# A fused attention and MoE kernel: the first gated products for one chunk of 128 tokens at a time

## The chip, the cores and the metric

The kernel runs on one core of one Trainium2 chip. The metric is the device time of one execution in microseconds (us). The engines are PE (matmul; its weight loads are listed apart as PEld), DVE and ACT (elementwise work, and the only ones here that empty PSUM), POOL (a few copies and products) and SP (issues the DMAs). Each engine takes its instructions in order; they meet at semaphores.

## The reference, cut to what matters

A delta-rule attention over 768 tokens, 4 batches, 8 heads of size 48, and then a gated MoE of one expert on all 3072 tokens:

```python
for t in range(S):
    kt, vt, bt = (k_n[:, :, t], v[:, :, t], beta[:, :, t, None])
    y[:, :, t] = np.einsum('bhd,bhde->bhe', q[:, :, t], state)
    v_old = np.einsum('bhde,bhd->bhe', state, kt)
    state = state + bt[:, :, :, None] * np.einsum('bhd,bhe->bhde', kt, vt - v_old)
...
a = x @ w_a            # x: 3072 x 384, w_a and w_b: 384 x 1536
b = x @ w_b
return (a * b @ w_out).astype(np.float32)
```

`x` is the attention's `y` with the heads side by side.

## The kernel before

**Attention.** The 768 time steps are cut into 24 chunks of 32 steps; a chunk of all 4 batches is 128 tokens. Chunks go in groups of four. For a group there are the Gram products of keys and queries (`gram`, on PE from `rawb`), a triangular solve on DVE over all four chunks at once (`solve`: some thirty short multiplies and subtractions on `b`, finished by small PE products `b,tt`, `b,kb` and `wr,xn`), and then, chunk after chunk, the recurrence (`steps`): the state's product with keys and queries (`sh,rawb`), DVE's `f`, the product `f,tt`, ACT's `u`, the state's update `S_ps<-u,kb`, the output product `u,at`, and `y`. From `y`, DVE and ACT make the chunk's gated input, in two halves of 16 bits, in `xb`. Chunk 2s and chunk 2s+1 lie side by side in one slot of `xb`: 256 columns, a pair.

**MoE.** The hidden width of 1536 is cut into 12 weight blocks of 128. A block is loaded from `in_w`, unpacked on DVE (one TENSOR_SCALAR and two SCALAR_TENSOR_TENSOR on 128x1152), scaled and split into high and low parts: for the first four blocks by small PE products with `zi`, `neg` and `negr` and ACT casts, for the others on DVE. A unit is one block for one pair (`moe`): two groups of nine matmuls, 128x128 weights against 256 columns, give a and b in one PSUM bank; ACT copies a (`a`), DVE multiplies (`g`), ACT and DVE split the product (`ghl`). Two units later (`LAG`), `moe_out` multiplies `ghl` with the block of `w_out`: three matmuls of 384 columns for each chunk, into one PSUM bank per chunk, which stays taken until the last block of the run.

The units of the first two pairs are queued in runs (`QUEUE`): pair 0 with blocks 0 to 5, pair 1 with 0 to 5, then the same with 6 to 8 and 9 to 11; partial sums lie in `acc`. Later pairs take all 12 blocks in one run. So the first unit needs chunk 0 and chunk 1.

**What sets the order.** The code only records operations (`Plan.add`). `Plan.order` then runs a list scheduler (`Plan.pack`) six times, with priorities from each pass's result run backwards, and keeps the best order by its own estimate; `issue` writes that order out. It hands out the six PSUM banks and models instruction fetch and the TensorE clock by fixed numbers. Where it sees PE idle in the first 60 us it writes fillers, matmuls on a tile of ones (`ones`, line 477), up to `SHY` ns ahead of the next operation. All recorded work has line 486, so the names of tiles tell the operations apart.

Of the kernel before, what the change touches and what calls it, by code (L numbers as in the profile page):

```python
# [17 lines left out]
AF = mybir.ActivationFunctionType  # L18
ALU = mybir.AluOpType
# [4 lines left out]
DM, FF = 384, 1536  # L24
C = 32
NCH = S // C
P = 128
KR = 112
GROUPS = [list(range(i, i + 4)) for i in range(0, NCH, 4)]
NG = len(GROUPS)  # L30
NFC = FF // P
# [8 lines left out]
def boost(o):  # L40
    return BOOST.get(o.stream + ("_pe" if o.stream == "moe" and o.eng == "PE" else ""), 0.0)
# [1 line left out]

EARLY = [(0, "k"), (2, "k"), (0, "r")]
NEXT = [(2, "r", 2, "k"), (0, "v", 0, "r"), (2, "v", 2, "r"), (0, "w", 2, "r"), (1, "w", 0, "v"), (2, "w", 2, "v"), (4, "k", 0, "w"), (4, "r", 1, "w"), (4, "v", 2, "w")]
QUEUE = [(0, [0, 1, 2, 3, 4, 5]), (1, [0, 1, 2, 3, 4, 5]), (0, [6, 7, 8]), (1, [6, 7, 8]), (0, [9, 10, 11]), (1, [9, 10, 11])]
LAG = 2
LEAD = 4
URGENCY = {"first": 5000, "prep0": 5000, "solve0": 5000, "steps0": 5000, "w0": 3000, "w1": 2500, "w": 1500, "prep1": 3000, "solve1": 3000, "steps1": 3000, "prep": 200, "solve": 600, "steps": 500, "moe": 800, "moe_pe": 300}
# [11 lines left out]
class Plan:  # L61
# [350 lines left out]
    MOVE = (1200.0, 1300.0)  # L412
    LOADED = (3500.0, 5600.0)
    BEGIN, IDLE, SINCE, UNTIL = 63, (50.0, 440.0), 1200.0, 60e3
    SHY, KEEP, GAIN, HEAT = 1500.0, 0.41, 0.42, (3.0, 430.0)

    def fetch(self, t, n, took, pos, come, dma):
        slip, come, known = 0.0, come[:], len(come)
# [14 lines left out]
    def order(self):  # L433


        self.link()
        ops = self.ops
        self.first = {o.eng: o for o in reversed(ops)}
        self.users = {}
        for o in ops:  # L440
            for b in o.banks:
                self.users[b] = self.users.get(b, 0) + 1
        self.succ = [[] for _ in ops]
        self.pred = [[] for _ in ops]
        for i, o in enumerate(ops):
            for j in o.deps:
                late = self.late(ops[j], o)
                self.succ[j].append((i, late))
                self.pred[i].append((j, late))
        pri, best = [o.pri - boost(o) - 1e12 * (o.stream == 'load') for o in ops], None  # L450
        for _ in range(self.PASSES):
            found = self.pack(pri)
            if found is None:
                break
            at, stop, done, total, bind = found
            if best is None or total < best[0]:
                best = (total, at, stop, done, bind)
            _, stop, _, total, _ = self.pack([-t for t in stop], True)
            pri = [k - 1e12 if o.stream == 'load' else total - t - boost(o) for k, (o, t) in enumerate(zip(ops, stop))]
        for o, o.at, o.end in zip(ops, best[1], best[2]):  # L460
            pass
        self.bind, self.fill = best[4]
        return best[3]
# [26 lines left out]
def tile_kernel(ctx, tc, kqt, kn, vn, begin, w, out):  # L490
    nc = tc.nc
    plan = Plan(nc)
    V, A, T, G, SP = (
        plan.engine(e, o)
        for e, o in (("DVE", nc.vector), ("ACT", nc.scalar), ("PE", nc.tensor), ("POOL", nc.gpsimd), ("SP", nc.sync))
    )
# [7 lines left out]
    def ring(p, name, n, shape, dt):  # L504
        tiles = [p.tile(shape, dt, name=f"{name}_{i}") for i in range(n)]
        used = [0]

        def get():
            used[0] += 1
            return tiles[(used[0] - 1) % n]  # L510

        get.tiles = tiles
        return get

    plan.pool = [psp.tile([P, 512], F32, name=f"bank{i}") for i in range(6)]
    att, abr, opr = (partial(lambda kind, n: plan.bank(kind, next(n)), kind, count()) for kind in range(3))
# [10 lines left out]
    ghr = ring(cst, "ghl", LAG + 1, [P, 2, 256], F32R)  # L527
    ar = ring(cst, "a", 2, [P, 256], F32)
    gr = ring(cst, "g", 2, [P, 256], F32)
# [70 lines left out]
    def halves(fc):  # L600
        return wh[:, fc].bitcast(F16).rearrange("p (l a) -> p l a", l=2), wo[:, fc]
# [49 lines left out]
    def wpart(m, j, fc, hl):  # L651
        o = (m * 3 + j) * P
        return halves(fc)[0][:, hl, o : o + P]

    facs = [None] * NCH
    xsub = [None] * (NCH // 2)
# [25 lines left out]
    acc = [one(f"acc{i}", [P, DM]) for i in range(4)]  # L682
# [26 lines left out]
    grams, rest = {}, []  # L709
# [316 lines left out]
    pend = []  # L1026
# [2 lines left out]
    def mm(*a, **k):  # L1029
        T.matmul(*a, **k)  # L1030

    def moe(s, fcs):
        xt = xsub[s]
        for fc in fcs:
            assert fc in whole
            ab = abr().rearrange("p (a n) -> p a n", a=2)

            plan.behind = set(opened[-1:] + closed[-LEAD:][:1] * (len(closed) >= LEAD))
            opened.append(len(plan.ops))
            for m in range(2):  # L1040
                n = 0
                with plan.group():
                    for j in range(3):
                        for l, rr in ((0, 0), (0, 1), (1, 0)):
                            T.matmul(
                                ab[:, m, :], wpart(m, j, fc, l), xt[:, rr, j, :], start=(n == 0), stop=(n == 8)
                            )
                            n += 1
            asb = ar()
            A.copy(asb, ab[:, 0, :])  # L1050
            g32 = gr()
            V.tensor_mul(g32, ab[:, 1, :], asb)
            ghl = ghr()
            A.copy(ghl[:, 0], g32)
            V.tensor_sub(ghl[:, 1], g32, ghl[:, 0].bitcast(F32))
            closed.append(len(plan.ops) - 1)
            pend.append((s, fc, ghl, fc == fcs[0], fc == fcs[-1]))
            if len(pend) > LAG:
                moe_out(*pend.pop(0))
            yield  # L1060

    ops = {}

    def moe_out(s, fc, ghl, first, last):
        if first:
            ops[s] = [opr()[:, 0:DM] for i in range(2)]
        for i in range(2):
            with plan.group():
                for n, (l, k) in enumerate(((0, 0), (0, 1), (1, 0))):
                    T.matmul(  # L1070
                        ops[s][i],
                        ghl[:, l, i * P : (i + 1) * P],
                        halves(fc)[1][:, k],
                        start=(first and n == 0),
                        stop=(last and n == 2),
                    )
            if last:
                c = 2 * s + i
                part = acc[c] if s < 2 else None
                final = fc == NFC - 1  # L1080
                ob = obs[c % 2] if final else part
                if part is not None and c in started:
                    V.scalar_tensor_tensor(ob, ops[s][i], facs[c], part, op0=ALU.mult, op1=ALU.add)
                else:
                    A.activation(ob, ops[s][i], AF.Copy, scale=facs[c])
                    started.add(c)
                if final:
                    SP.dma_start(out[c], ob)
# [12 lines left out]
    def run_all(gen):  # L1101
        for _ in gen:
            pass
# [5 lines left out]
    def merge(*streams):  # L1109

        todo = [[g_, n_, 0] for g_, n_ in streams]
        total_n = max(n_ for _, n_ in streams)
        for i in range(total_n):
            for t in todo:
                while t[2] * total_n <= i * t[1] and t[2] < t[1]:
                    next(t[0], None)
                    t[2] += 1
        for t in todo:
            if t[0] is not moes:
                run_all(t[0])  # L1120

    queue = []

    def moe_stream():
        while True:
            if queue:
                yield from moe(*queue.pop(0))
            else:
                yield

    moes = lab("moe", moe_stream())

    ws = [lab(f"w{i}", weights(i)) for i in range(len(PARTS))]
# [23 lines left out]
    run_all(ws[1])  # L1157
    queue.extend(QUEUE)
    run_all(ws[2])
# [8 lines left out]
    for g in range(1, NG):  # L1168
        n = len(GROUPS[g])
        if g < 2:  # L1170
            merge((st[g], 3 * n), (moes, 4 * n), (pr[g + 1], 2 + len(GROUPS[g + 1])))
        elif g + 1 < NG:
            next(pr[g + 1])
            merge((st[g], 3 * n), (moes, 4 * n))
            merge((pr[g + 1], 2 + len(GROUPS[g + 1])), (moes, 2))
        else:
            merge((st[g], 3 * n), (moes, 4 * n))
        queue.extend((s, list(range(NFC))) for s in range(GROUPS[g][0] // 2, GROUPS[g][-1] // 2 + 1))
        if g + 1 < NG:
            merge((sv[g + 1], 8), (moes, 8))  # L1180
    while queue:
# [3 lines left out]
    while pend:  # L1185
        moe_out(*pend.pop(0))
# [69 lines left out]
```

## Time and profile before

| | |
|---|---|
| median of 3 runs | 656.53 us (655.1 to 660.78) |
| the profiled execution | 658.43 us |
| its span, first to last instruction | 656.6 us |
| granted TensorE clock, mean | 0.961 |
| PE busy | 625.9 us of the span |
| first gated product of a pair | 77.76 us |
| state product of chunk 8 begins | 196.54 us |

A row of the profile has the line, the engine and the operation, then out<-in by tile names, partitions and elements; x counts instructions. In a list of groups busy us and mean ns follow, then the engine's idle time before them and what ended it; "issue" means that the profile shows nothing the engine waited for. In a timeline a row begins with start and length in us, and the square bracket is idle time before it. A row of stretches has begin and end, length, busy us and count for each engine, the granted clock of TensorE (1.00 is full), the busy share of the DMA engines and GB/s. One call of an fp32 matmul is two matmuls and two weight loads in the trace.

### The profile page before, as it was taken

Reading aid. Unit: us, or ns where it says so; the run is one execution under the profiler, and the core shown is the slowest. Engines: PE = TensorE matmul, PEld = TensorE weight load, DVE = VectorE, ACT = ScalarE, POOL = GpSimd, SP = SyncE. Lnnn points to the kernel's source line nnn. Section 1 sums busy time; section 2 is a strip of 40 time slices with the busy share of each in tenths; the row PEclk is TensorE's granted clock in tenths of the full one; section 3 lists DMA queues with packets and bytes.
Section 4 is the critical chain, followed back from the end, with each engine's and each line's share of the span. In section 5 each row is a group of like instructions: output and inputs, shape, how many; then the busy total and the mean of one; then the engine's idle time right before and its main releaser. Section 6 shows DMA issues by size and latency. Waiting matters only on the chain.

```text
span 656.6 us, 26617 instructions
## 1 busy us (share of the span) xinstructions
PE 625.9 (95%) x12184; PEld 535.3 (82%) x12184; DVE 404.8 (62%) x1059; ACT 270.4 (41%) x599; POOL 25.7 (4%) x62
## 2 busy tenths in 40 slices
PE   7788999998999999999999999999999999999997
PEld 6575688777788887888878888888888888888887
DVE  5796699768666995448965389754686533222222
ACT  4245684245445634323373234733324333232322
POOL 0000000000012200000020000200000000000000
PEclk8858799879999999999999999999999999999999
DMA  7837202212276000004300033000000000000000
GB/s 252 312 130 272 80 4 74 80 70 76 70 226 190 19 2 27 4 14 134 108 2 29 4 115 112 26 4 28 3 1 26 4 3 25 1 25 2 25 1 24
DMA packets 19824, 42.78 MB, mean 65 GB/s; under 512 B 1280, under 2 KB 4352, under 8 KB 19712
## 3 DMA queue, kind: packets, MB, share of 16 engines
q1 hardware_dynamic: 19712, 41.08, 18.9%
q8 instruction: 95, 1.56, 1.0%
q14 instruction: 17, 0.14, 0.1%
HBM read 36.36 MB, written 4.72 MB: 63 GB/s over the span
## 4 chain that ended last, share of the span: by engine, by line
PE 78%; DVE 12%; ACT 4%; issue 3%; ACTq 0%
PE bank L486 75%; DVE b L486 3%; PE S_ps L486 3%; DVE tmp L486 2%; ACT sqf L486 2%; DVE wh L486 1%; DVE ghl L486 1%; DVE late L486 1%; DVE g L486 1%; ACT ghl L486 1%; ACT tt L486 1%; ACT a L486 0%; DVE sc L486 0%; DVE ss L486 0%; DVE s L486 0%
## 5 line engine op out<-in xcount | busy, mean ns | idle before, releaser
L486 PEld LDWEIGHTS <-wh 128*128 128x128 f16 x2592 | 241.2, 98 | 50.6 <-issue 22.4
L486 PE MATMUL bank<-xb,wh 128*128 128x256 f16 x2160 | 259.8, 273 | 2.2 <-issue 2.2
L486 PE MATMUL bank<-wo,ghl 128*128 128x384 f32 x864 | 192.3, 356 | 0.6 <-issue 0.6
L486 PEld LDWEIGHTS bank<-wo,ghl 128*128 128x128 f32 x864 | 145.2, 190 | 4.8 <-issue 1.6
L486 ACT COPY a<-bank 128x256 f32<-128x256 f32 x144 | 53.6, 372 | 195.4 <-PE bank L486 195.3
L486 DVE TENSOR_TENSOR g<-bank,a 128x256 f32<-128x256 f32 x144 | 60.8, 422 | 114.8 <-ACT a L486 113.5
L486 DVE TENSOR_TENSOR ghl<-g,ghl 128x256 fp32r<-128x256 f32 x144 | 62.3, 432 | 35.0 <-ACT ghl L486 33.8
L486 ACT CAST ghl<-g 128x256 fp32r<-128x256 f32 x144 | 58.1, 404 | 60.4 <-DVE g L486 59.6
L486 PE MATMUL bank<-late,wh 128*128 128x256 f16 x432 | 52.0, 273 | 1.2 <-ACT u L486 1.2
L486 DVE TENSOR_TENSOR b<-b,tmp 128x31 f32<-128x31 f32 (+20 forms) x154 | 50.9, 330 | 2.8
L486 DVE TENSOR_TENSOR tmp<-b,b 128x31 f32<-128x31 f32 (+20 forms) x154 | 50.8, 330 | 2.9
L486 ACT ACTIVATE y<-bank,sc 128x384 f32<-128x384 f32 x24 | 14.0, 582 | 45.1 <-PE bank L486 42.8
L486 DVE SCALAR_TENSOR_TENSOR y<-bank,sc,y 128x384 f32<-128x384 f32 x23 | 14.2, 616 | 29.6 <-ACT y L486 29.6
L486 PEld LDWEIGHTS bank<-rawb 48*32 48x32 f32 x1280 | 21.2, 117 | 7.7 <-issue 3.7
L486 PE MATMUL bank<-rawb 48*32 48x64 f32 x1280 | 24.0, 232 | 3.3 <-DMA rawb<-in_kqt 3.3
L486 DVE TENSOR_TENSOR b<-bank,dc 128x256 f32<-128x256 f32 x24 | 14.5, 605 | 20.6 <-PE bank L486 17.1
L486 PEld LDWEIGHTS bank<-sh,rawb 48*64 48x64 f32 x1216 | 21.3, 144 | 6.7 <-issue 5.3
L486 PEld LDWEIGHTS bank<-f,tt 32*32 32x32 f32 x1472 | 17.9, 107 | 9.3 <-issue 5.5
L486 PE MATMUL bank<-sh,rawb 48*64 48x48 f32 x1216 | 23.9, 229 | 0.7 <-issue 0.7
L486 PE MATMUL bank<-u,at 32*32 32x48 f32 x1536 | 22.3, 206 | 1.9 <-issue 1.9
L486 PE MATMUL bank<-f,tt 32*32 32x48 f32 x1472 | 21.2, 206 | 2.5 <-issue 1.4
L486 DVE TENSOR_TENSOR f<-vnb,bank 128x384 f32<-128x384 f32 x38 | 19.9, 548 | 5.7 <-PE bank L486 5.1
(120 smaller groups left out, 552.8 us busy)
## 6 DMA issues: line engine op xcount, KB each, us to landing
late<-in_w SPq DMA_DIRECT2D x10, 1152.0 KB, 6.8
rawb<-in_kqt SPq DMA_DIRECT2D x12, 512.0 KB, 3.7
out<-late SPq DMA_DIRECT2D x24, 192.0 KB, 1.9
rawb<-in_kqt SPq DMA_DIRECT2D x4, 1024.0 KB, 7.0
vnb<-in_vn SPq DMA_DIRECT2D x10, 384.0 KB, 3.2
kb<-in_kn SPq DMA_DIRECT2D x9, 384.0 KB, 3.9
wh<-in_w SPq DMA_DIRECT2D x2, 1152.0 KB, 9.7
late<-in_kqt SPq DMA_DIRECT2D x4, 512.0 KB, 3.7
```

Of the source, the lines that this page charges most:

```text
L486: fn(*(self.place(a, lease) for a in args), **{k: self.place(a, lease) for k, a in kw.items()})
```

## The change

The queue now holds units of a pair, a block and the chunks (`parts`) that it covers. The first four units are half units: chunk 0 with blocks 0 and 1, then chunk 1 with the same two; the rest go on in pairs as before, blocks 2 to 5 of pair 0 first. A half unit has the same eighteen weight tiles against 128 columns, half the columns in `a`, `g` and `ghl`, and a second product for its one chunk. `moe_out` keeps its sums by chunk in place of by pair, opened by a chunk's first unit of a run and closed by its last. Matmuls of 128x256 on `xb` fall from 2160 to 2124, and 72 of 128x128 come; the second products stay 864.

Besides, `SHY` goes from 1500 to 500: fillers may reach nearer to the operation behind them. The lines in `order` change nothing: they would act where a pass of the scheduler finds no order, and all six find one.

```diff
-QUEUE = [(0, [0, 1, 2, 3, 4, 5]), (1, [0, 1, 2, 3, 4, 5]), (0, [6, 7, 8]), (1, [6, 7, 8]), (0, [9, 10, 11]), (1, [9, 10, 11])]
+BOTH = (0, 1)
+QUEUE = [[(0, 0, (0,)), (0, 1, (0,)), (0, 0, (1,)), (0, 1, (1,))] + [(0, b, BOTH) for b in (2, 3, 4, 5)]]
+QUEUE += [[(s, b, BOTH) for b in bs] for s, bs in ((1, range(6)), (0, (6, 7, 8)), (1, (6, 7, 8)), (0, (9, 10, 11)), (1, (9, 10, 11)))]
...
-    SHY, KEEP, GAIN, HEAT = 1500.0, 0.41, 0.42, (3.0, 430.0)
+    SHY, KEEP, GAIN, HEAT = 500.0, 0.41, 0.42, (3.0, 430.0)
...
             if found is None:
-                break
-            at, stop, done, total, bind = found
-            if best is None or total < best[0]:
+                stop, total = [float(k) for k in range(len(ops))], 0.0
+            else:
+                at, stop, done, total, bind = found
+            if found is not None and (best is None or total < best[0]):
+                best = (total, at, stop, done, bind)
+            if 0 is None or total < best[0]:
                 best = (total, at, stop, done, bind)
...
-    def moe(s, fcs):
-        xt = xsub[s]
-        for fc in fcs:
+    def moe(units):
+        for u, (s, fc, parts) in enumerate(units):
+            xt = xsub[s]
             assert fc in whole
-            ab = abr().rearrange("p (a n) -> p a n", a=2)
+            lo, n_t = parts[0] * P, len(parts) * P
+            ab = abr().rearrange("p (a n) -> p a n", a=2)[:, :, 0:n_t]
...
-                                ab[:, m, :], wpart(m, j, fc, l), xt[:, rr, j, :], start=(n == 0), stop=(n == 8)
+                                ab[:, m, :],
+                                wpart(m, j, fc, l),
+                                xt[:, rr, j, lo : lo + n_t],
+                                start=(n == 0),
+                                stop=(n == 8),
                             )
...
-            pend.append((s, fc, ghl, fc == fcs[0], fc == fcs[-1]))
+            mine = [2 * s + i for i in parts]
+            rest = [2 * v[0] + i for v in units[u + 1 :] for i in v[2]]
+            pend.append((fc, ghl, [(c, c not in sums, c not in rest) for c in mine]))
...
-    def moe_out(s, fc, ghl, first, last):
-        if first:
-            ops[s] = [opr()[:, 0:DM] for i in range(2)]
-        for i in range(2):
+    def moe_out(fc, ghl, work):
+        for i, (c, first, last) in enumerate(work):
+            if first:
+                ops[c] = opr()[:, 0:DM]
...
-        queue.extend((s, list(range(NFC))) for s in range(GROUPS[g][0] // 2, GROUPS[g][-1] // 2 + 1))
+        queue.extend([(s, fc, (0, 1)) for fc in range(NFC)] for s in range(GROUPS[g][0] // 2, GROUPS[g][-1] // 2 + 1))
```

The scheduler sorts the whole program anew, so much stands elsewhere. On ACT, around chunk 1's `u`, which the recurrence waits for (`wh`, `wo` and `sqf,sw` are the weight blocks, `sh` and `y` the recurrence), the order was

```order
L486 COPY u_74<-bank_63 128x384
L486 ACTIVATE wr_94<-bank_61 128x128
L486 CAST wh<-bank_62 128x384
L486 CAST wh<-bank_61 128x384
L486 ACTIVATE sqf,sw_138<-wh 128x768
L486 CAST wo<-bank_62 128x384
L486 COPY sh_76<-S_ps 112x768
L486 ACTIVATE y_96<-bank_64,sc_127 128x384
```

and now, on the same engine at the same place, it is

```order
L491 COPY u_74<-bank_63 128x384
L491 CAST wh<-bank_61 128x384
L491 COPY a_101<-bank_62 128x128
L491 CAST wh<-bank_63 128x384
L491 CAST ghl_98<-g_103 128x128
L491 ACTIVATE sqf,sw_138<-wh 128x768
L491 CAST wo<-bank_62 128x384
L491 COPY a_102<-bank_61 128x128
L491 CAST ghl_99<-g_104 128x128
L491 COPY sh_76<-S_ps 112x768
L491 ACTIVATE y_96<-bank_64,sc_127 128x384
```

Chunk 0's half units with blocks 0 and 1 now end ahead of chunk 2's `sh`, and `wr` of chunk 3's solve has moved behind chunk 2's `u`.

On PE, where the solve of group 1 (chunks 4 and 5: `b_3,tt_85` and `b_3,tt_86`) begins, second products stood between its parts:

```order
L486 MATMUL bank_64<-wo,ghl_99 128x384 x3
L486 MATMUL bank_63<-b_3_71,tt_85 32x16 x32
L486 MATMUL bank_62<-wo,ghl_99 128x384 x3
L486 MATMUL bank_66<-b_3_71,tt_86 32x16 x32
L486 MATMUL bank_63<-b_3_71,kb 128x256
L486 MATMUL bank_64<-wo,ghl_100 128x384 x3
L486 MATMUL bank_66<-b_3_71,kb 128x256
L486 MATMUL bank_63<-wr_93,xn 16x16 x32
```

and now the same engine has at this place

```order
L491 MATMUL bank_62<-wo,ghl_98 128x384 x3
L491 MATMUL bank_61<-wo,ghl_98 128x384 x3
L491 MATMUL bank_65<-b_3_71,tt_85 32x16 x32
L491 MATMUL bank_66<-b_3_71,tt_86 32x16 x32
L491 MATMUL bank_65<-b_3_71,kb 128x256
L491 MATMUL bank_62<-wo,ghl_99 128x384 x3
L491 MATMUL bank_66<-b_3_71,kb 128x256
L491 MATMUL bank_61<-wo,ghl_99 128x384 x3
```

The two `b,tt` groups have moved together; nine gated matmuls follow, and then the groups `wr_93,xn` and `wr_94,xn`, one right behind the other. Ahead of them PE now has six units of pair 0 and six of pair 1, where it had six and four.

At the start of PE's program the fillers stood as

```order
L477 MATMUL bank_66<-ones 128x256 x6
L486 MATMUL bank_61<-rawb 32x64 x32
L486 MATMUL bank_62<-rawb 32x64 x32
L486 MATMUL bank_63<-rawb 32x64 x32
L486 MATMUL bank_64<-rawb 32x64 x32
L477 MATMUL bank_66<-ones 128x256 x20
```

and are now

```order
L482 MATMUL bank_66<-ones 128x256 x7
L491 MATMUL bank_61<-rawb 32x64 x32
L491 MATMUL bank_62<-rawb 32x64 x32
L482 MATMUL bank_66<-ones 128x256
L491 MATMUL bank_63<-rawb 32x64 x32
L491 MATMUL bank_64<-rawb 32x64 x32
L482 MATMUL bank_66<-ones 128x256 x21
```

One filler more at either end and one between the Gram products of chunks 1 and 2; two others have moved in between the small products `sw,ones` of the first weight blocks, which makes 31 in place of 26.

More of the change, by code (lines that the diff above doesn't have):

```diff
@@ L1045, in moe @@
                             T.matmul(
-                                ab[:, m, :], wpart(m, j, fc, l), xt[:, rr, j, :], start=(n == 0), stop=(n == 8)
+                                ab[:, m, :],
[3 more added lines that the diff above has]
+                                stop=(n == 8),
                             )
                             n += 1
-            asb = ar()
+            asb = ar()[:, 0:n_t]
             A.copy(asb, ab[:, 0, :])
-            g32 = gr()
+            g32 = gr()[:, 0:n_t]
             V.tensor_mul(g32, ab[:, 1, :], asb)
-            ghl = ghr()
+            ghl = ghr()[:, :, 0:n_t]
             A.copy(ghl[:, 0], g32)
@@ L1056, in moe @@
             closed.append(len(plan.ops) - 1)
-            pend.append((s, fc, ghl, fc == fcs[0], fc == fcs[-1]))
+            mine = [2 * s + i for i in parts]
+            rest = [2 * v[0] + i for v in units[u + 1 :] for i in v[2]]
+            pend.append((fc, ghl, [(c, c not in sums, c not in rest) for c in mine]))
+            for c in mine:
+                sums.setdefault(c, None)
+                if c not in rest:
+                    over.add(c)
             if len(pend) > LAG:
                 moe_out(*pend.pop(0))
+            for c in over:
+                del sums[c]
+            over.clear()
             yield
-    ops = {}
-    def moe_out(s, fc, ghl, first, last):
-        if first:
-            ops[s] = [opr()[:, 0:DM] for i in range(2)]
-        for i in range(2):
+    sums, over, ops = {}, set(), {}
+    def moe_out(fc, ghl, work):
+        for i, (c, first, last) in enumerate(work):
+            if first:
+                ops[c] = opr()[:, 0:DM]
             with plan.group():
@@ L1070, in moe_out @@
                     T.matmul(
-                        ops[s][i],
+                        ops[c],
                         ghl[:, l, i * P : (i + 1) * P],
@@ L1077, in moe_out @@
             if last:
-                c = 2 * s + i
-                part = acc[c] if s < 2 else None
+                part = acc[c] if c < 4 else None
                 final = fc == NFC - 1
@@ L1082, in moe_out @@
                 if part is not None and c in started:
-                    V.scalar_tensor_tensor(ob, ops[s][i], facs[c], part, op0=ALU.mult, op1=ALU.add)
+                    V.scalar_tensor_tensor(ob, ops[c], facs[c], part, op0=ALU.mult, op1=ALU.add)
                 else:
-                    A.activation(ob, ops[s][i], AF.Copy, scale=facs[c])
+                    A.activation(ob, ops[c], AF.Copy, scale=facs[c])
                     started.add(c)
@@ L1126, in moe_stream @@
             if queue:
-                yield from moe(*queue.pop(0))
+                yield from moe(queue.pop(0))
             else:
```

## The prediction

> **What bounds the kernel now.** I read the page from the top: busy time by engine, the slices, the chain that ended last; then PE's busy time and granted clock in stretches cut where the clock changes; then PE's timeline where it stood still.
>
> ```profile
> PE 625.9 (95%) x12184; PEld 535.3 (82%) x12184; DVE 404.8 (62%) x1059; ACT 270.4 (41%) x599; POOL 25.7 (4%) x62
> PE   7788999998999999999999999999999999999997
> PEclk8858799879999999999999999999999999999999
> PE 78%; DVE 12%; ACT 4%; issue 3%; ACTq 0%
> q8 instruction: 95, 1.56, 1.0%
> L486 PEld LDWEIGHTS <-wh 128*128 128x128 f16 x2592 | 241.2, 98 | 50.6 <-issue 22.4
> L477 PE MATMUL bank<-ones 128*128 128x256 f32 x52 | 16.2, 484 | 1.1 <-DVE ones L486 1.1
> ```
>
> PE carries 78% of the chain and is busy 95% of the span: time can come only from PE's idle time, from PE at half clock, or from PE work left out. The slices put both losses in the first third. The stretches (us, PE busy, PEld, DVE, ACT, POOL, clock, DMA share, GB/s):
>
> ```profile
> 48.00:54.40 6.40, 6.40 (x136) 3.93 (x136) 2.62 (x12) 5.00 (x9) 0.00 (x0) 0.50 0.94 338
> 64.20:68.10 3.90, 1.19 (x9) 0.47 (x4) 2.06 (x7) 1.62 (x4) 0.00 (x0) 0.99 0.80 236
> 68.10:74.90 6.80, 6.76 (x72) 3.93 (x72) 5.23 (x9) 3.88 (x9) 0.00 (x0) 0.50 0.27 101
> 74.90:118.20 43.30, 42.90 (x1072) 37.05 (x1071) 38.21 (x119) 27.91 (x61) 0.00 (x0) 1.00 0.09 30
> 118.20:122.70 4.50, 3.12 (x135) 2.36 (x134) 4.50 (x8) 0.89 (x4) 0.00 (x0) 0.99 0.01 4
> 122.70:126.10 3.40, 3.40 (x72) 2.60 (x71) 3.40 (x4) 0.37 (x1) 0.00 (x0) 0.50 0.03 5
> 126.10:132.90 6.80, 6.31 (x158) 4.59 (x157) 2.72 (x10) 3.01 (x9) 0.00 (x0) 1.00 0.80 278
> 132.90:139.70 6.80, 5.45 (x140) 4.69 (x140) 2.19 (x7) 2.49 (x5) 0.00 (x0) 0.50 0.20 76
> 139.70:196.50 56.80, 54.30 (x1330) 46.23 (x1328) 41.31 (x84) 28.85 (x62) 2.25 (x10) 1.00 0.35 106
> 196.50:656.60 460.10, 450.20 (x7965) 393.04 (x7964) 260.18 (x703) 174.09 (x397) 20.77 (x39) 1.00 0.11 35
> ```
>
> And PE's timeline at the two kinds of loss, with DVE's row on which each chunk's gated input is complete:
>
> ```profile
> 48.17 0.56 DVE L486 TENSOR_TENSOR xb<-yt,xb 128x384 f16<-128x384 f32 x1
> 62.50 0.93 PE L486 MATMUL S_ps<-u,kb 32*48 32x48 f32 x64
> 63.37 0.88 PE L486 MATMUL bank<-u,at 32*32 32x48 f32 x64
> 66.78 0.34 PE L486 MATMUL bank<-wh,neg 128*128 128x384 f16 x1 [2.54 <-issue]
> 69.28 0.56 DVE L486 TENSOR_TENSOR xb<-yt,xb 128x384 f16<-128x384 f32 x1 [1.01 <-ACT xb L486]
> 77.76 2.13 PE L486 MATMUL bank<-xb,wh 128*128 128x256 f16 x18
> ...
> 106.53 2.14 PE L486 MATMUL bank<-xb,wh 128*128 128x256 f16 x18
> 108.42 1.30 PE L486 MATMUL bank<-wo,ghl 128*128 128x384 f32 x6
> ...
> 118.23 0.74 PE L486 MATMUL bank<-b,tt 32*32 32x16 f32 x64
> 118.90 0.79 PE L486 MATMUL bank<-wo,ghl 128*128 128x384 f32 x3
> 119.62 0.70 PE L486 MATMUL bank<-b,tt 32*32 32x16 f32 x61
> 121.70 0.24 PE L486 MATMUL bank<-b,tt 32*32 32x16 f32 x3 [1.38 <-issue]
> ```
>
> Chunk 0's input is complete at 48.7, chunk 1's at 69.8, and the first gated product runs at 77.76: for 29 us there is MoE work that could run, and doesn't. The stalls "issue" stand in the middle of a row of equal matmuls, so they wait for no data. 12184 matmuls and as many weight loads in 95 packets of the instruction queue are 256.5 instructions a packet: PE's instructions come in blocks of 128 pairs. The 128 pairs that end in the stall at 121.70 (64, 3, 61) need some 2.1 us of PE and took 3.47; those from 62.50 (64 and 64) need 1.75 and took 4.28, with DMA 0.80 busy. So PE can't get through a block faster than about 3.5 us, or 4.3 with transfers about, and after such a stall the clock fell to 0.50. The Trainium skill (Runtime: NRT & Kernel Launch, Instruction fetch mechanics) also has blocks of 256 instructions, but calls their fetch mostly hidden; the 1.38 us show that it isn't where tiles are small.
>
> **The change, part by part.** I compare PE up to one mark: the first product of chunk 8's step, 196.5 us before. Ahead of it both orders hold the same PE work, but for half groups and fillers. So the gain is the losses before the mark that vanish, less what is added and what is lost anew.
>
> Recovered, 64.2 to 74.9: idle 2.71 and 0.04, and half of 6.76 at clock 0.50, 3.38; together 6.1 us. In the new order the two groups that stalled (S_ps, u,at of chunk 1) stand between half groups and second products, so their block is long, PE has work where it waited, and nothing there lets the clock fall.
>
> Recovered, 118.2 to 196.5: idle 1.38, 0.49, 1.35 and 2.50, half clock 1.70 and 2.73; together 10.2 us. That all of it goes is not granted: what comes in its place is below.
>
> Added, half groups: 36 matmuls of 256 columns become 72 of 128. The wide one takes 105 ns (18 from 106.53 to 108.42), 3.8 us for 36. A narrow pair costs between half of that, 53 ns (0 more), and the 98 ns of its weight load (3.3 us more). As loads overlap matmuls in these rows I take the middle, 75 ns: 72 x 75 = 5.4, 1.6 more. The Trainium skill (TensorE: Matmul & The Clock Gate, Back-to-back issue gap) has some 81 ns for such a pair; the sum would be 0.4 us worse. No narrow pair is in this trace. The first nine run before 54.4 at clock 0.50: 9 x 75 = 0.7 more (0.5 to 0.9).
>
> Added, five more fillers on `ones` (two matmuls each). Three lie before 32 us, where PE waits for DVE anyway. Two stand between the small products of `sw` near 47 us, 2 x 2 x 484 ns = 1.9 us at most, where PE sat idle 0.9: I take 0.2 (0 to 1.0).
>
> Added waits: a half group waits for ACT's last cast of its half of the weight block, and behind it on PE, which runs in order, stands chunk 1's recurrence (f,tt and S_ps). For block 0's first half this cast is
>
> ```profile
> 52.90 0.48 ACT L486 CAST wh<-bank 128x384 f16<-128x384 f32 x1
> ```
>
> done at 53.4, and two other matmuls stand between it and the group, so I cost no wait; without them it would be the 0.5 us of the cast.
>
> Added on ACT and DVE: eight half evacuations on each, between the conversions of weight blocks 1 to 6. In this row DVE has 8.3 us free:
>
> ```profile
> 59.30:102.40 43.10, 39.45 (x1160) 30.23 (x1159) 34.78 (x85) 30.32 (x64) 0.00 (x0) 0.92 0.21 68
> L486 DVE TENSOR_SCALAR wh<-late x3: 751/753/754, 88.0 to 143.3; 128x1152 int32<-128x1152 int32 x3
> L486 DVE SCALAR_TENSOR_TENSOR wh<-late,wh x6: 1349/1352/1364, 98.3 to 146.3; 128x1152 int32<-128x1152 int32 x6
> L486 DVE TENSOR_TENSOR g<-bank,a 128x256 f32<-128x256 f32 x144 | 60.8, 422 | 114.8 <-ACT a L486 113.5
> ```
>
> Ahead of group 1's solve the order now has, on DVE, all of weight block 7 (0.75 + 2 x 1.35) and part of 8 (0.75 + 1.35), and two more units (4 x 0.43): 7.3 us, plus small change. That fills the 8.3. I cost it at nothing because PE brings chunk 7's Gram product some 6 us later as well, with the MoE work that it pulled ahead; if DVE idles as before, it is the second rival. The weight loads keep their order on SP, and POOL's gates come after the mark.
>
> Lost anew, blocks of 128 pairs that the new order fills with small tiles, at 3.5 us each less the PE time in them. Chunk 2's step and chunk 3's solve together (f,tt, b,tt, S_ps, u,at): two blocks with 4.9 us of work, 2.0. The first two Gram products with the last of chunk 3: 0.7. The solve of chunks 4 and 5 (two groups wr,xn in a row): 1.7 us of work, with weight block 10 on its way, 2.2. Chunk 5's update with chunk 6's state product: 1.7. Others 0.5. And one window of half clock after the solve, as 122.7 to 126.1 now: 1.7. Together 8.8; nothing, if the small groups don't fall into one block, and some 14 with 4.3 us for each and a second window.
>
> The sum: 6.1 + 10.2 - 1.6 - 0.7 - 0.2 - 8.8 = 5.0 us. After the mark PE idles 9.9 us of 460 in both orders, by my estimate. The profiled execution has a span of 656.6 in 658.43 us; it would have 651.6 in 653.4. The median of the runs is 656.53, 1.9 below that execution; less 5.0 it is 651.5.
>
> **Rivals.** One: the new short blocks don't bind, since they lie between long ones, and the clock stays up. For it: from 74.9 to 118.2 PE idles 0.4 us of 43 with small groups in it. Against: every stretch after it. Then up to 16.3 - 2.5 = 13.8 is gained, 643; with half of the 8.8, 647. By the skill's rule that fetches are hidden it would be this.
>
> Two: DVE becomes the bound. If it idles 8.3 us in its stretch as before, the solve of group 1 starts some 5 us after PE could use it, and the lead is given back: 655 to 658. For it: the DVE sum; against: DVE was 38.2 of 43.3 us busy from 74.9 to 118.2 without holding PE.
>
> Three, slower: weight loads 8 to 11 fall on the short blocks. The 128 pairs that end in the stall at 135.00 begin 34 pairs ahead of 129.58; with DMA 0.80 busy they took some 5.8 us, though 4.4 us of work were in them:
>
> ```profile
> 129.58 0.79 PE L486 MATMUL bank<-wo,ghl 128*128 128x384 f32 x3
> 135.00 1.03 PE L486 MATMUL bank<-f,tt 32*32 32x48 f32 x41 [1.35 <-issue]
> late<-in_w SPq DMA_DIRECT2D x10, 1152.0 KB, 6.8
> ```
>
> Two blocks for each of four loads at 5.8 in place of 3.5, half of it hidden, are 9.2 us, and two windows more 3.4: 664. It ends slower than before from 5.0 us on, four of the eight blocks.
>
> **How the numbers follow.** The forecast, 651.5 with a range of its own of 648 to 656, has 0.5; the first rival 0.25, the second 0.14, the third 0.11. A measurement of this kernel can tell about 1% from no change, that is 650.0 and 663.1. Faster by over 1% are the first rival and the lower quarter of the forecast, 0.37; slower, most of the third, 0.09; within it 0.54. The range of 8 in 10 runs from 645, deep in the first rival, to 658, the end of the second.
>
> **What would show it.** Right: PE runs 128-column matmuls from about 53 us, the clock stays 1.00 from 54 to beyond 100 us, the 2.54 us stall is gone, the mark comes near 191.5, and stalls on "issue" stand in the small groups near 78, 130 and 160 us. Wrong: half groups over 0.9 us each; PE waiting on DVE ahead of group 1's solve; half clock in three or more windows after 100 us; or a mark that comes early with the end unmoved.

## The result and the profile after

| | before | after |
|---|---|---|
| median of 16 runs | 656.27 us (652.92 to 660.78) | 660.87 us (654.07 to 667.38) |
| ratio, 95% interval | 1 | 1.005 (1.0026 to 1.0073) |
| profiled execution, span | 656.6 us | 660.2 us |
| first product of chunk 8's step, "the mark" | 196.54 us | 190.46 us |
| from the mark to the end | 460.1 us | 469.7 us |

Half a per cent slower, within the 1% of no change. The forecast was 651.5, with a range to 658. The mark came where it was forecast (191.5); behind it 9.7 us went. The ratios, here and below, leave out executions more than 1.5% above the fastest of their kernel (here the one of 667.38 us).

The page of after: PE's share of busy time in 40 slices, its granted clock, and the group `u,at`, which ends each chunk's recurrence, with its idle time at the end:

```profile
PE   7889999789989998899989999999999999999997
PEclk7958999989999999989989999999999999999999
L491 PE MATMUL bank<-u,at 32*32 32x48 f32 x1536 | 23.9, 209 | 5.8 <-issue 5.8
```

The same group before:

```profile
L486 PE MATMUL bank<-u,at 32*32 32x48 f32 x1536 | 22.3, 206 | 1.9 <-issue 1.9
```

The clock's five in the third slice stays; the seven that before had in its fifth slice (65 to 82 us) is gone, and new eights stand in the 18th and the 21st (281 to 297 and 330 to 347 us), where before had nines. "Issue" ahead of `u,at` went from 1.9 to 5.8 us. The stretches of after (us, PE busy, PEld, DVE, ACT, POOL, clock, DMA share, GB/s):

```profile
54.40:106.00 51.60, 50.52 (x1402) 40.78 (x1402) 48.15 (x115) 37.02 (x82) 0.00 (x0) 1.00 0.32 110
131.50:138.40 6.90, 5.70 (x145) 4.05 (x148) 6.65 (x14) 2.38 (x5) 0.00 (x0) 0.51 0.01 2
...
281.70:285.20 3.50, 3.50 (x57) 2.73 (x49) 1.55 (x4) 0.51 (x1) 0.00 (x0) 0.51 0.00 0
339.70:343.20 3.50, 3.38 (x99) 2.55 (x90) 1.84 (x5) 1.27 (x2) 0.00 (x0) 0.51 0.02 5
...
190.46:660.20 469.74, 453.95 (x7964) 394.95 (x7964) 263.21 (x708) 175.54 (x399) 22.81 (x42) 0.99 0.12 37
```

Behind the mark PE has 7964 matmuls in both traces. It is busy for 453.95 us where it was 450.20, since two stretches run at half clock (half of 3.50 and 3.38 is 3.4), and idle for 15.8 us where it was 9.9. These 3.75 and 5.9 are the 9.7 us. Of the idle time, stalls of over 0.25 us inside groups of equal matmuls make 7.1 us (4.1 before), and waits of over 0.25 us that end with DVE, ACT or POOL 4.7 (2.2 before). PE's timeline of after shows the half groups, the waits and three stalls ahead of the mark and two losses behind it:

```profile
52.10 1.12 PE L491 MATMUL bank<-xb,wh 128*128 128x128 f16 x9
53.06 0.86 PE L491 MATMUL bank<-wh,zi 128*128 128x384 f32 x2
...
69.00 1.17 PE L491 MATMUL bank<-xb,wh 128*128 128x128 f16 x18
70.00 0.86 PE L491 MATMUL bank<-wh,zi 128*128 128x384 f32 x2
...
106.72 1.31 PE L491 MATMUL bank<-wo,ghl 128*128 128x384 f32 x6 [1.02 <-ACT a L491]
121.13 1.33 PE L491 MATMUL bank<-b,tt 32*32 32x16 f32 x128 [0.76 <-DVE g L491]
...
130.90 0.39 PE L491 MATMUL bank<-xb,wh 128*128 128x256 f16 x2 [2.39 <-issue]
132.70 1.33 PE L491 MATMUL bank<-wo,ghl 128*128 128x384 f32 x3 [1.29 <-ACT ghl L491]
148.46 0.49 PE L491 MATMUL bank<-xb,wh 128*128 128x256 f16 x3 [1.78 <-issue]
164.47 0.16 PE L491 MATMUL bank<-sw,ones 128*128 128x1 f32 x1 [0.90 <-issue]
190.46 0.75 PE L491 MATMUL bank<-sh,rawb 48*64 48x48 f32 x37 [0.65 <-DMA rawb<-in_kqt]
...
263.15 1.10 PE L491 MATMUL bank<-rawb 48*32 48x64 f32 x64
264.18 0.93 PE L491 MATMUL S_ps<-u,kb 32*48 32x48 f32 x64
265.04 0.61 PE L491 MATMUL bank<-u,at 32*32 32x48 f32 x37
266.81 0.53 PE L491 MATMUL bank<-u,at 32*32 32x48 f32 x27 [1.16 <-issue]
...
338.05 1.10 PE L491 MATMUL bank<-rawb 48*32 48x64 f32 x64 [1.60 <-POOL late L491]
```

Chunk 9's step before, from the same view:

```profile
267.95 1.10 PE L486 MATMUL bank<-rawb 48*32 48x64 f32 x64
268.97 0.93 PE L486 MATMUL S_ps<-u,kb 32*48 32x48 f32 x64
269.84 0.88 PE L486 MATMUL bank<-u,at 32*32 32x48 f32 x64
270.65 1.37 PE L486 MATMUL bank<-xb,wh 128*128 128x256 f16 x11
```

The same 192 matmuls take 2.7 us before and 4.1 after; after, the third group breaks in two at its 37th. That looks like the stalls at the end of a block of 256 PE instructions that the prediction read, but behind the mark. Two theories: the scheduler re-sorted the late work into a worse order; or the order is as good, and 46 more pairs of weight load and matmul (36 of the half groups, 10 of the five fillers) move every later block. "Place" below means the number of PE instructions ahead, modulo 256: "old places" are those of before, "new places" lie 46 pairs on.

### The profile page after: what moved, and what is told of

It reads as the page before. It is cut to its first block, busy times and chain, and to the rows that moved or that the text cites. A ratio compares the mean times of both kernels' runs of the same rounds, so it can differ in the third digit from the quotient of the medians.

```text
span 660.2 us, 26696 instructions
## 1 busy us (share of the span) xinstructions
PE 627.3 (95%) x12230; PEld 536.3 (81%) x12230; DVE 406.8 (62%) x1063; ACT 271.8 (41%) x603; POOL 26.5 (4%) x62
## 4 chain that ended last, share of the span: by engine, by line
PE 77%; DVE 12%; DMA 4%; issue 3%; ACT 3%; POOL 0%; SPq 0%; POOLq 0%; ACTq 0%
PE bank L491 74%; DVE b L491 3%; PE S_ps L491 3%; DVE tmp L491 2%; DMA late<-in_kqt 1%; DVE g L491 1%; DVE ghl L491 1%; DMA rawb<-in_kqt 1%; ACT sqf L491 1%; DMA late<-in_vn 1%; DVE wh L491 1%; ACT ghl L491 1%; DMA kb<-in_kn 1%; DVE ss L491 0%; ACT a L491 0%
## 5 line engine op out<-in xcount | busy, mean ns | idle before, releaser
L491 PE MATMUL bank<-xb,wh 128*128 128x256 f16 (+1 forms) x2196 | 263.0, 273 | 5.3 <-issue 4.2
L491 DVE TENSOR_TENSOR g<-bank,a 128x256 f32<-128x256 f32 (+1 forms) x146 | 61.1, 418 | 126.0 <-ACT a L491 124.6
L491 ACT COPY a<-bank 128x256 f32<-128x256 f32 (+1 forms) x146 | 53.9, 369 | 191.6 <-PE bank L491 191.3
L491 DVE TENSOR_TENSOR ghl<-g,ghl 128x256 fp32r<-128x256 f32 (+1 forms) x146 | 62.8, 430 | 36.8 <-ACT ghl L491 34.9
L491 ACT CAST ghl<-g 128x256 fp32r<-128x256 f32 (+1 forms) x146 | 58.5, 401 | 65.5 <-DVE g L491 64.9
L491 PE MATMUL bank<-u,at 32*32 32x48 f32 x1536 | 23.9, 209 | 5.8 <-issue 5.8
L491 PEld LDWEIGHTS bank<-u,at 32*32 32x32 f32 x1536 | 19.7, 109 | 8.9 <-issue 7.6
L491 ACT COPY sh<-S_ps 112x768 f32<-112x768 f32 x23 | 18.3, 795 | 11.8 <-PE S_ps L491 11.8
```

Of the source, the lines that this page charges most:

```text
L491: fn(*(self.place(a, lease) for a in args), **{k: self.place(a, lease) for k, a in kw.items()})
```

## The experiments

**Order, places, or a debt?** In the first kernel each engine and queue has the changed kernel's order up to the mark and the old one from there; the second is its mirror. `TAIL` is a table of 1707 operations (1700 in the second); PSUM banks are handed out anew along it.

```diff
-        return best[3]
+        return self.splice(best[3])
+
+    def splice(self, done):
+        tail = set(TAIL)
+        done = [i for i in done if i not in tail] + TAIL
...
```

> The changed kernel up to the first product of chunk 8's step; from there on every engine and queue has the old kernel's order. Theory (order): the 9.7 us that the changed kernel loses after that mark belong to the order into which the rest was re-sorted. Then the mark stays near 190.5 us, the rest takes some 460 us as before, and the time is 649 to 653 us, a ratio near 0.992. Rival (places of the blocks): they belong to the places at which PE's blocks of 128 pairs now begin, 46 pairs on; these places are as in the changed kernel, so the rest takes some 470 us in the old order too, and the time is 658 to 662. A second rival (work that was put off: the first part hands a debt to the rest) gives 658 to 662 as well, with waits on DVE or DMA right behind the mark.

> The opposite: the old kernel up to the mark, and from there on the changed kernel's order. Order theory: mark near 196.5 us, rest some 470, the time 664 to 667, a ratio near 1.014. Rival (places of the blocks): the places are the old ones, the rest takes some 460 us, and the time is 655 to 658. Rival (debt): there is none, 655 to 658.

New head and old tail: 664.51 us, ratio 1.0116 (1.009 to 1.0141). Behind the mark:

```profile
189.80:662.70 472.90, 451.76 (x7965) 393.06 (x7964) 260.67 (x705) 174.32 (x398) 21.17 (x40) 1.00 0.11 35
```

Old head and new tail: 659.84 us, 1.0034 (1.0008 to 1.006):

```profile
196.82:658.90 462.08, 450.34 (x7965) 393.19 (x7964) 259.94 (x702) 174.86 (x397) 20.61 (x38) 1.00 0.11 34
```

The order theory, which was my first, falls: the old order takes 472.9 us behind the new head, the new one 462.1 behind the old. The loss goes with the head, and that leaves its places, or a debt: work that the head puts off. (Both medians lie some 2 us above the ranges that I had given to places.)

**Places alone.** The fillers are matmuls on a tile of ones whose result nobody reads. Cut in two, three or four along their columns, they bring more pairs into the queue in about the same time, and no other instruction changes its order.

```diff
+CUTS = [2] * 21 + [3] * 10
...
+                        cols = 256 // CUTS.pop(0)
+                        for c in range(0, 256 // cols * cols, cols):
+                            self.nc.tensor.matmul(
+                                self.pool[-1][:, c : c + cols],
+                                one,
...
```

> The old kernel with its own order; of its 26 fillers 23 are cut in two of half the columns, so that 46 more pairs stand in PE's queue from about 30 us on and all later blocks of 256 instructions begin where the changed kernel's do. Theory (places of the blocks): the rest after the mark takes 467 to 472 us in place of 460.1, with more idle time inside groups, and the mark moves too; 660 to 670 in all. Rival (debt of the first part): the first part is the old one, the rest stays at 459 to 462, 655 to 658 in all.

> The changed kernel with its own order and 82 more pairs, cut out of its 31 fillers (21 in two, 10 in three), so that later blocks begin where the old kernel's do (46 + 82 = 128). Places: the rest takes 460 to 464 us, as this order took behind the old first part (462.1). Debt: 468 to 471, as in the changed kernel.

> The changed kernel up to the mark, the old order behind it (472.9 us behind the mark in the first such run), and 82 more pairs cut out of the fillers: behind the mark every engine has the old order and PE's blocks the old places. Places: the rest takes 459 to 462 us, the mark stands between 189 and 193, and the time is 650 to 655. Debt: the rest takes 470 to 474 us again, 662 to 665.

The old kernel at new places: 662.02 us, 1.0088 (1.006 to 1.0117). Its stretch behind the mark, and chunk 9's `u,at`:

```profile
189.25:658.30 469.05, 451.36 (x7965) 393.24 (x7964) 259.84 (x702) 173.97 (x397) 20.20 (x38) 1.00 0.11 34
```

```profile
261.93 0.53 PE L491 MATMUL bank<-u,at 32*32 32x48 f32 x29
263.87 0.61 PE L491 MATMUL bank<-u,at 32*32 32x48 f32 x35 [1.41 <-issue]
```

The changed kernel at old places: 644.87 us, **0.9829 (0.9796 to 0.9863)**, against before. Its stretch, the row of the page for `u,at`, and chunk 9's step:

```profile
181.38:642.20 460.82, 450.22 (x7965) 392.80 (x7964) 261.62 (x705) 174.81 (x399) 22.03 (x41) 1.00 0.12 36
```

```profile
L496 PE MATMUL bank<-u,at 32*32 32x48 f32 x1536 | 21.9, 204 | 1.7 <-issue 1.7
```

```profile
253.22 1.10 PE L496 MATMUL bank<-rawb 48*32 48x64 f32 x64
254.24 0.93 PE L496 MATMUL S_ps<-u,kb 32*48 32x48 f32 x64
255.11 0.88 PE L496 MATMUL bank<-u,at 32*32 32x48 f32 x64
255.92 1.31 PE L496 MATMUL bank<-wo,ghl 128*128 128x384 f32 x6
```

The stall came into the old order and went out of the new one, each time with the places. The median of the changed kernel falls by 16 us. Its mark comes at 181.38 us, 9.1 earlier than in after; but 3.1 of these are there by 54 us, where both traces have the same product of `wh` and `zi` (54.40 in after, 51.30 here), and the clock, at half in both from some 33 us on, is up again at 40.8 us here and at 53.1 in after. Whether the places did that too is not shown. The third kernel, new head and old tail at old places: 651.09 us, 0.9922 (0.9891 to 0.9953).

```profile
184.26:649.50 465.24, 452.35 (x7964) 394.71 (x7964) 261.24 (x706) 174.59 (x399) 22.13 (x42) 0.99 0.12 37
```

```profile
193.99 4.00 PE L594 MATMUL bank<-xb,wh 128*128 128x256 f16 x18 [4.42 <-DVE g L594]
```

That is 5 us more than in the old kernel, and one wait on DVE right behind the seam takes 4.42 of them. I had expected 459 to 462 for the rest and a mark between 189 and 193; it came at 184.26, so that the time lay in its range by two misses that cancel. So here there is a debt at the seam of the two orders; but 7.7 of the 12.8 us by which the first spliced kernel was worse than before behind the mark are gone by moving places.

**A whole block more.** If it is the places, 128 pairs must change nothing; if it is the finer fillers, they must do as well as 82. Same edit, with other lists of cuts.

> The changed kernel with 128 more pairs cut out of its fillers (29 in three, 2 in four): a whole block, so that behind the fillers every block of 256 instructions begins at the same matmul as in the changed kernel, while the fillers are cut even finer than in the run with 82. Theory (places): the rest after the mark goes back to 467 to 472 us (460.8 with 82). Rival (the finer fillers themselves, by more and shorter matmuls or a warmer clock): the rest stays at 459 to 463.

> The old kernel with 128 more pairs cut out of its fillers (14 in three, 12 in four): old order, old places. It stands beside the run of the changed kernel with 82, which has the same places and cut fillers too. Places: the rest is 459 to 462 us as before. For the mark: if finer fillers alone make the half clock before 54 us shorter, it comes at 187 to 192 and the time is 648 to 653; then the changed order is worth the difference to 181.4 and 644.9. If it stays at 194 to 197, the whole gain of that run is the changed order's at good places.

> The changed kernel with 64 more pairs (30 fillers cut in two, one in three): half a block on. Places: the rest lies between the two known values of this order, 469.8 at 0 and 460.8 at 82 more pairs, and not above 472; since the step of each group of recurrence is 1.5 blocks long, I expect 460 to 467. Finer fillers: 459 to 463.

> The changed kernel with 104 more pairs (10 fillers cut in two, 21 in three). Places: 22 pairs beyond the best known place and 24 short of the bad one; the rest is 460 to 467 us, the time 644 to 655. Finer fillers: as with 82, 643 to 646.

The changed kernel with 128 more pairs: its profiled execution has 662.3 us; the other five took 679 to 681, of which there is no trace; their granted clock, 0.984 to 0.995, is above the 0.974 of the profiled one, so a slower clock is not what makes them long. The stretch behind the mark and chunk 9's `u,at`:

```profile
190.58:660.50 469.92, 454.17 (x7965) 395.10 (x7964) 261.30 (x705) 175.00 (x398) 21.35 (x40) 0.99 0.11 35
```

```profile
263.70 0.61 PE L496 MATMUL bank<-u,at 32*32 32x48 f32 x37
265.51 0.53 PE L496 MATMUL bank<-u,at 32*32 32x48 f32 x27 [1.19 <-issue]
```

469.9 us again and the stall again at the 37th matmul. The mark stands at 190.58 as against 190.46, which is partly luck: this execution is 2.2 us behind at 54 us, and one stall of after, the 1.78 at 148.46, isn't in it. For the rest behind the mark, finer fillers don't explain the gain; places do. The old kernel with 128 more pairs, 658.12 us, 0.9996 (0.9962 to 1.003), is the old kernel again, but for four of its twelve executions, which took 670 to 675:

```profile
197.53:659.10 461.57, 452.19 (x7965) 394.52 (x7964) 260.10 (x702) 174.04 (x397) 20.42 (x38) 1.00 0.11 34
```

With 64 the changed kernel takes 653.27 us, 0.9923 (0.9897 to 0.9949); its profiled execution, 660.15, is the longest of twelve, with 474.4 us behind the mark where I had expected 472 at most; the other eleven, 650.16 to 654.42, have no trace. With 104 it takes 649.12, 0.9882 (0.9832 to 0.9932), the rest being 462.1 and the mark 185.0, though it is 0.5 us behind after at the product near 54 us. So one order of one kernel takes between 644.9 and 660.9 us, with nothing changed but how often its fillers are cut (0, 64, 82 and 104 more pairs):

| order | places | mark | rest | rest without PE busy |
|---|---|---|---|---|
| old | old | 196.5 (197.5 with 128) | 460.1 (461.6) | 9.9 (9.4) |
| old | new | 189.3 | 469.1 | 17.7 |
| new | new | 190.5 (190.6 with 128) | 469.7 (469.9) | 15.8 (15.8) |
| new | old | 181.4 | 460.8 | 10.6 |

The table also shows what the change is worth at equal places: by the medians some 11 us at the old ones (644.87 against 656.27), some 1 us at the new ones (660.87 against 662.02).

**One part of the change alone.** The scheduler sorts everything anew in both, and the places are others too: 36 pairs on for the half units, 10 for the fillers.

```diff
-    SHY, KEEP, GAIN, HEAT = 500.0, 0.41, 0.42, (3.0, 430.0)
+    SHY, KEEP, GAIN, HEAT = 1500.0, 0.41, 0.42, (3.0, 430.0)
```

> The changed queue of units with the old SHY of 1500 (26 fillers, not 31). The planner sorts everything anew. Order theory: the mark comes 3 to 6 us ahead of the old one, and the rest takes whatever its own order costs, between 458 and 472 us; the time is between 650 and 664 and need not be the changed kernel's. If the loss after the mark belongs to the half units themselves, the rest takes 469 to 471 us again and the time is 659 to 662.

The second has the old queue and the same line the other way round.

> The old queue of units with SHY at 500 (31 fillers, not 26). Everything is sorted anew here too. If the first 2 us by which the changed kernel is ahead at the product on zi near 46 us are the fillers', this kernel has them as well (46.1 in place of 48.2), and no half groups. Order theory: the rest after the mark takes its own time, 458 to 472 us, and the whole 652 to 667; if re-sorting costs nothing, it is 654 to 657.

Half units alone: 655.91 us, 0.9987 (0.9967 to 1.0008); fillers alone: 651.47, 0.9919 (0.9889 to 0.9949). Both leave 24 pairs fewer behind the mark. The fillers alone, first `zi` product and last stretch:

```profile
45.76 1.63 PE L486 MATMUL bank<-wh,zi 128*128 128x384 f32 x2
```

```profile
191.85:651.60 459.75, 447.47 (x7941) 389.99 (x7940) 258.85 (x702) 173.57 (x396) 22.29 (x41) 1.00 0.12 36
```

That product stands at 48.24 us before, at 46.09 after, at 47.72 with half units alone: the early 2 us come with the lower SHY, by its fillers or by the order that it brings. The mark came at 193.3 and 191.9, so either part alone is enough for an early mark. To set the parts side by side, both were moved to the old places:

> Fillers alone (SHY 500, no half units), with 118 more pairs cut out of the fillers, 10 + 118 = 128: the old kernel's places of the blocks. If the half groups earn the early mark, it stands at 189 to 196 us here and the time is 650 to 657; if the re-sorting that SHY brings does, it comes at 180 to 186 as in the changed kernel with 82 (181.4), 641 to 648.

> Half units alone (SHY 1500), with 92 more pairs, 36 + 92 = 128: again the old kernel's places. If the half groups earn the early mark, it comes at 180 to 187 us, 641 to 650; if not, 190 to 196 and 651 to 658. In both runs the rest, in an order planned for other places, is 459 to 468.

Half units alone: 647.82 us, 0.9858 (0.9821 to 0.9895):

```profile
190.88:644.00 453.12, 446.77 (x7941) 389.59 (x7940) 258.26 (x699) 173.71 (x395) 21.64 (x40) 1.00 0.12 35
```

Fillers alone: six executions between 646.18 and 663.99, too far apart for a ratio. In the profiled one, 660.13 us, the clock stays at half until 70 us, though PE is busy; the mark comes at 203.5, later than I had expected by either account:

```profile
9.00:70.00 61.00, 59.15 (x1063) 53.76 (x1064) 33.44 (x95) 19.65 (x40) 2.28 (x9) 0.50 0.51 182
203.50:658.30 454.80, 446.51 (x7941) 389.57 (x7940) 258.71 (x702) 173.34 (x396) 21.85 (x41) 1.00 0.12 36
```

So half units alone gain at these places, but by the rest (453.1) rather than by the mark (190.9), against what I had expected of them. That does not make the gain theirs: the fillers alone have nearly the same rest there (454.8), and their shortest execution, 646.18, is nearly as short. How much each part of the change is worth stays open: every kernel in which a part is left out is sorted anew, and what an order is worth depends on its places.

**Tell the scheduler.** It counts places by matmuls and weight loads alone. The edit lets its blocks be a little shorter:

```diff
+    BLOCK = 255.4
...
-        for b in range(-(-pos // 256), -(-(pos + n) // 256)):
-            at = t + took * (b * 256 - pos) / n
+        for b in range(math.ceil(pos / self.BLOCK), math.ceil((pos + n) / self.BLOCK)):
+            at = t + took * (b * self.BLOCK - pos) / n
```

> The changed kernel with one number of its planner changed: blocks of 255.4 of its instructions rather than 256, since the 47 to 61 semaphore and drain instructions that the traces show on PE's queue stand in the same blocks (every stall inside a group in the traces of before and after falls at 192 of 256, if these are counted). Everything is sorted anew. Places: with nearly right places the late stalls inside groups (7.1 us behind the mark) shrink to 2 to 5 and the rest to 460 to 466, 649 to 658 in all. Debt: the rest stays at 468 to 471.

655.87 us, 0.9997 (0.9974 to 1.0021): better than after by the medians, no better than before. Chunk 13's step:

```profile
357.92 0.70 PE L493 MATMUL bank<-u,at 32*32 32x48 f32 x45
360.09 0.44 PE L493 MATMUL bank<-u,at 32*32 32x48 f32 x19 [1.48 <-issue]
```

The rest, 463.8 us, has 42 pairs fewer in it, and the stalls of over 0.25 us inside groups sum to 11.8 us where I had expected 2 to 5. A miss: nearer places in the plan are not enough for it to avoid the stalls. Why was not tried.

## Why the prediction was wrong

**The step that failed** is one sentence: "After the mark PE idles 9.9 us of 460 in both orders, by my estimate." It was 9.9 and 15.8, and 3.4 us of half clock came on top. The prediction had the mechanism, blocks of 128 pairs at whose end PE can stall, and used it on the order ahead of the mark. It did not ask what 46 more pairs do to all blocks behind it, where the recurrence of every later group lies in rows of 192 small matmuls. That is shown: old order and new places lose the same 9 us, new order and old places do not, and a whole block more leaves the rest as it was in the execution that was profiled.

**The price of a block** was too plain as well. It was 3.5 us for every block, 4.3 with transfers about; but in the trace of before the blocks that end in a stall inside a group took from 2.7 to 5.8 us, and in the changed kernel with 82 more pairs the 128 from 433.76 us on, all small, took 1.88 us without a stall. So a short block can stall and need not; what decides it, beside the place, no run here settles.

**The mark was right, but for half of a reason.** Recovered, 64.2 to 74.9: as forecast; the 2.54 us stall is gone and the clock is 1.00 from 54.4 to 106. Recovered, 118.2 to 196.5, 10.2 us: the stalls at 121.7, 135.0 and 155 us are gone, but they go from the old order as well when it is moved by 46 pairs (mark at 189.25). Lost anew, 8.8 us: the three stalls in the rows above, 5.07, and half clock from 131.5 to 138.4, half of 5.70 or 2.85, are 7.9. Two of the stalls come when they were forecast, near 130 and 160, though not inside the recurrence's small groups, and none at 78. These losses go with the new places: at the old ones the same order has none of the three stalls and no half clock after 54 us. Four waits that no term had take 3.7 us more: 1.02 (by its place at the end of a block too), 0.76, 1.29 and 0.65 in the rows above. So 16.3 recovered and 2.1 gained by 46 us, less 0.7 for half groups, 7.9 and 3.7, are the 6.1 us of the mark. That 5.0 came so near to it is partly luck, since what the sum left out on either side, 2.1 and 3.7, partly cancels. In the list of new losses two subtractions are off as well: two blocks less 4.9 us are 2.1, not 2.0, and a block less 1.7 us is 1.8 or, at 4.3, 2.6, not 2.2.

**Half groups** were over-priced. Eighteen narrow matmuls take 1.00 us from row to row (69.00 to 70.00), 55.6 ns each where I took 75: 0.2 us for all in place of 1.6, and 0.5 for the first nine, which took 0.96 us at half clock (52.10 to 53.06) and would take 0.50 at full, in place of 0.7. The 81 ns of the Trainium skill (TensorE: Matmul & The Clock Gate, Back-to-back issue gap) don't hold in this row; the 55.6 ns that the same page gives for back-to-back matmuls (Wait — 56ns, not 53.3ns?) do.

**Fillers** cost nothing that shows, and 2.1 us were gained by 46 us with the lower SHY, which no term had.

**The rivals.** That short blocks don't bind is wrong for many of them in every trace here, though not for all. The Trainium skill's rule is that fetch is mostly hidden (Runtime: NRT & Kernel Launch, Instruction fetch mechanics). In the trace of after that holds at most of the ends of its 95 blocks, but 14 stalls inside groups sum to 14.3 us. DVE did not take the lead back: ahead of group 1's solve (121.13 us) PE waited 0.76 us for it, and the mark kept the lead. The third had the right sign and the right mechanism at the wrong place, loads ahead of the mark. Three of the signs of being wrong that it had named came: a wait on DVE ahead of that solve, three windows of half clock after 100 us (from 131.5, 281.7 and 339.7), and an early mark with the end unmoved. The sum: 6.1 us gained ahead of the mark (forecast 5.0), 9.7 lost behind it (forecast 0): the span is 3.6 us longer.

## What to carry to other kernels

Where an engine runs near the rate at which its instructions arrive, adding or removing a few instructions moves every later block. That alone was worth some 9 us behind the mark here, and some 6 to 9 ahead of it, about as much as the change itself at its best. Before judging an edit of such a kernel, look in which block its late small groups fall, or time it at several places: dummy matmuls cut finer in idle time turn the queue by any number of pairs. The best kernel found, 1.7% faster than before, is the changed one with 82 pairs of that kind; it owes this to the new order and to a number of pairs that the next edit spoils.

## What the hardware showed that was not expected

Blocks count every PE instruction. In five traces (before, after, old at 46, changed at 82 and 128) 59 stalls of over 0.25 us on "issue" stand inside a group of equal matmuls, and all 59 fall where twice the pairs plus the semaphore and drain instructions ahead come to 192 or 193 modulo 256. The stall at 121.7 us before has 2519 pairs and 18 such instructions ahead of it, 5056, or 19 x 256 + 192. Without those (61 in the trace of before, 47 after) the place drifts by 25 pairs from the first to the last stall of before, by 19 in after.

Finer fillers did not act alike: with 118 pairs cut out of them the profiled execution kept half clock for 61 us of nearly unbroken work (59.15 us busy, in that run's row above), and with 128 five of six executions took 17 us more than the sixth, at a higher granted clock. No run here tells why.
